# Retention and SoLU block on one Trainium2 core: state products as 64x64 tiles in two ordered passes, column means from fp32 column tiles, and a new written-out order

## Chip, cores and metric

The kernel runs on one core of one Trainium2 chip. The metric is the device time of one execution in microseconds (us). The kernel before was run three times: 220.96, 221.63 and 221.78 us, median 221.63 us.

## What is computed

```
q, k, v: [8 batches, 8 heads, 576 positions, 64], fp32
scores = (q @ k^T) / 8
ret    = scores * gamma_h ** (i - j)   for i >= j, else 0      gamma_h = 1 - 2 ** (-5 - h)
x      = (ret @ v), heads side by side                         [4608 tokens, 512]
h      = x @ w_in                                              [4608, 1024]
solu   = h * softmax(h)
ln     = (solu - mean) / sqrt(var + 1e-6) * g_ln               per token
out    = ln @ w_out                                            [4608, 512], fp32
```

The first half is causal attention with a decay for each head and no softmax, so what lies further back than the present window can be carried in a state of 64 x 64 numbers a head. The second half is a layer of two matrix products with SoLU and a layer norm between them. The mean of the layer norm is taken out of `w_out` (its columns are centred with weights `g_ln`), so that a token needs only its scale at the end.

## The kernel before

**Work units.** A window is 256 positions of one batch, or the last 64 positions of four batches (every ninth window). A window has two halves of four heads each; `i` numbers these 36 halves. A window gives two tiles of 128 tokens; `t` numbers these 36 tiles. Every step has a short name, and the engines execute these names in an order written out by hand in `ORDER` (L37 to L106), one string for each engine:

- SyncE (SP in the profile) issues all loads and stores: `ldq`, `ldk`, `ldv` (a quarter of a MB each; in the last windows four DMAs each), `lwi` (w_in) and `lwo` (w_out), `out` (two stores a tile, four in the last windows).
- GpSimd (POOL) scales and casts: `sq`, `sk` (L327), `cv` (L335), and keeps the states: `sm` (L458), `sc` (L467), and the scale of a token `rs` (L544, L545).
- TensorE: `T` transposes q and k into `ps["b"]`, `S` makes scores in `ps["a"]` (L402), `K` makes k^T v in columns 256 to 383 of `ps["x"]`, `I` adds what the state gives to columns 0 to 255 of `ps["x"]` and `V` adds what the window gives (all three end in `mm`, L368). `M1` is the product with w_in into `ps["h"]` (L483), `L` transposes solu into `ps["b"]` (L298, L552), `M2` is the product with w_out (L574). It writes the first half of `ps["a"]` for even tiles and the second for odd ones.
- VectorE: `mask` (L433), `sa` and `sd` (L447 to L454, states out of PSUM), `so` (solu, L510 and L515), `bn` (variance of even tiles), `wc` (centred w_out, L632).
- ScalarE: `qe` and `le` (transposes out of PSUM, L356 to L362, L561 to L563), `xe` (x out of PSUM, L473), `ex` (exponential, L501), `vs` (variance of odd tiles, L530), `oe` (result out of PSUM with its scale, L582), and `wg` (w_out times `g_ln` in fp16, L623, once for each of 8 chunks).

**PSUM.** There are four tiles of two banks: `h`, `a`, `b` and `x`. `h` holds one `M1` at a time, so the chain `M1`, `ex`, `so`, next `M1` runs in turn. `S` and `M2` share `a`.

**State products.** A state is kept as a 128 x 128 block-diagonal matrix for a pair of heads (`sbd`, zeroed off the diagonal at the start). `inter` (step `I`) multiplies it with 128 x 128 weights: two matmuls for the first window of a batch, four for the second, eight of 64 columns for the shared last window.

**Column means of w_out.** `WM` multiplies the eight fp16 chunks `w2g16` by a matrix of -1/1024 and accumulates (8 matmuls of 512 columns, L629); `wc` then reads the mean out of `ps["b"]`.

**Emission.** `order_ops` is a planner that walks the written orders with the costs in `DUR` and gives each step a planned start. The instructions are then emitted in the order of these planned starts; the semaphore waits follow from that program order. While TensorE has nothing to do before time `WARM`, `stir` (L745) fills in matmuls of zeros.

Of the kernel before, what the change touches and what calls it, by code (L numbers as in the profile page):

```python
# [9 lines left out]
FP = mybir.dt.float32  # L10
F16 = mybir.dt.float16
P = 128


DUR = dict(
    T=0.26, L=0.26, Tf=0.45, M1=1.73, M1a=1.3, M1b=0.44, M2=1.73, I=0.23, S=0.23, V=0.225, K=0.13, G=0.1, WM=1.73,
    qe=0.6, le=0.6, xe=0.61, ex=1.16, oe=0.72, vs=1.3, q2=0.24, wi=0.64, wib=0.5, wg=0.66, wgd=0.55, wc=0.66,
    cva=0.62, mask=1.24, sa=0.31, sd=0.31, so=1.26, sox=1.34, bn=1.64, sqd=0.72, gc=0.2,
    sq=1.06, sk=1.06, sm=0.42, sc=0.86, rs=1.0, cv=0.63,
    ld=0.5, ld4=2.6, ldw=0.6, out=1.1, out4=2.2, outz=0.55, lm=0.5,  # L20
)
MOVE = dict(ld=0.91, ld4=0.91, ldw=1.3, out=1.1, out4=1.1, outz=1.1, lm=0.4)
COUNT = dict(T=64, L=64, S=32, V=32, K=32, I=8, G=2, M1a=12, M1b=4)
# [4 lines left out]
START = dict(SP=2.3)  # L28
DMA_LAT, DMA_END = 0.1, 1.4
WARM = 31.0  # L30
NQ, NL = 9, 4
CA = (0,1,2,3,4,5)
WA = (0,1,2,3,4,5,6,7)
# [5 lines left out]
        "K0 G T0 S0 I0 V0 K1 T1 S1 I1 V1 T2 K2 S2 T3 I2 V2 K3 M1a S3 M1_0 I3 V3 K4 T4 M1_1 S4 I4 "  # L39
        "L0 V4 T5 L1 K5 S5 T6 M1_2 S6 I5 V5 K6 WM M1_3 I6 V6 K7 T7 S7 M1_4 T8 L2 M2_0 L3 M1_5 "  # L40
        "M2_1 I7 V7 K8 L4 T9 S8 M1_6 M2_2 I8 V8 K9 L5 T10 S9 M1_7 M2_3 I9 V9 K10 L6 S10 T11 M1_8 "
        "M2_4 I10 V10 K11 T12 L7 S11 M1_9 M2_5 I11 V11 K12 L8 S12 T13 M1_10 M2_6 I12 V12 K13 T14 "
        "L9 S13 M1_11 M2_7 I13 V13 K14 T15 S14 L10 M1_12 M2_8 I14 V14 K15 L11 T16 S15 M1_13 M2_9 "
        "I15 V15 T17 L12 S16 M1_14 M2_10 I16 V16 T18 L13 S17 M1_15 M2_11 I17 V17 K18 T19 S18 L14 "
        "M1_16 M2_12 I18 T20 V18 K19 L15 S19 M1_17 M2_13 I19 V19 K20 L16 T21 S20 M1_18 M2_14 I20 "
        "V20 L17 K21 T22 S21 M1_19 M2_15 I21 V21 K22 L18 T23 S22 M1_20 M2_16 I22 V22 L19 K23 T24 "
        "S23 M1_21 M2_17 I23 V23 K24 L20 T25 S24 M1_22 M2_18 I24 V24 T26 K25 L21 S25 M1_23 M2_19 "
        "I25 V25 K26 L22 T27 S26 M1_24 M2_20 I26 V26 K27 T28 L23 S27 M1_25 M2_21 I27 V27 K28 L24 "
        "S28 T29 M1_26 M2_22 I28 V28 T30 K29 L25 S29 M1_27 M2_23 I29 V29 K30 L26 S30 T31 M1_28 "
        "M2_24 I30 V30 K31 L27 T32 S31 M1_29 M2_25 I31 V31 K32 L28 S32 T33 M1_30 M2_26 I32 V32 "  # L50
        "K33 L29 T34 S33 M1_31 M2_27 I33 V33 L30 T35 S34 M1_32 M2_28 I34 V34 L31 S35 M1_33 I35 "
        "L32 V35 M2_29 L33 M1_34 M2_30 M2_31 L34 M1_35 M2_32 M2_33 L35 M2_34 M2_35"
    ),
    ACT=(
        "cv0 qe0 cv1 qe1 cv2 xe0 wi2a qe2 xe1 wi1a wi0a cv3 qe3 wi3a cv4 xe2 ex0 xe3 wg6 wg7 qe4 "
        "wg1 ex1 le0 cv5 wg0 qe5 le1 xe4 wg4 qe6 wg5 wg3 wg2 ex2 vs1 xe5 q20 ex3 qe7 vs3 ex4 le2 "
        "q21 xe6 qe8 oe0 le3 ex5 oe1 xe7 vs5 qe9 ex6 le4 oe2 q22 qe10 xe8 le5 ex7 oe3 xe9 le6 vs7 "
        "ex8 qe11 oe4 qe12 xe10 le7 ex9 oe5 xe11 q23 qe13 le8 ex10 q24 oe6 vs9 xe12 le9 ex11 qe14 "
        "oe7 xe13 qe15 le10 ex12 q25 oe8 vs11 qe16 xe14 ex13 le11 oe9 xe15 qe17 vs13 ex14 le12 "
        "oe10 xe16 q26 qe18 le13 ex15 oe11 xe17 qe19 le14 ex16 q27 oe12 vs15 xe18 qe20 ex17 le15 "  # L60
        "oe13 xe19 le16 vs17 ex18 qe21 oe14 q28 qe22 xe20 le17 ex19 oe15 xe21 qe23 le18 q29 ex20 "
        "oe16 vs19 xe22 qe24 ex21 le19 oe17 xe23 vs21 le20 ex22 qe25 oe18 qe26 q210 xe24 le21 "
        "ex23 q211 oe19 xe25 qe27 vs23 ex24 le22 oe20 qe28 le23 xe26 ex25 oe21 xe27 q212 le24 "
        "vs25 ex26 qe29 oe22 le25 xe28 qe30 ex27 oe23 xe29 q213 vs27 qe31 ex28 le26 oe24 le27 "
        "xe30 qe32 ex29 oe25 xe31 qe33 vs29 ex30 le28 oe26 le29 qe34 q214 xe32 ex31 oe27 xe33 "
        "le30 qe35 ex32 oe28 le31 xe34 ex33 le32 xe35 q215 oe29 vs31 ex34 le33 oe30 vs33 oe31 "
        "q216 ex35 q217 le34 oe32 vs35 oe33 le35 oe34 oe35"
    ),
# [722 lines left out]
```

## Time and profile before

| | |
|---|---|
| runs | 220.96, 221.63, 221.78 us; median 221.63 |
| the profiled execution | 221.71 us; span of its instructions 219.6 us; the rest lies around the span |
| busy share of the span | TensorE 92%, ScalarE 72%, GpSimd 65%, VectorE 64% |
| mean granted TensorE clock | 0.992 |
| instructions of the program | 10216 |
| read from HBM, written | 32.71 MB, 9.44 MB |

Times in the profile are microseconds from the start of the span. In the groups of the page a line reads: source line, engine, operation, output and input names, shapes, count; then busy time and mean ns of one; then the idle time of the engine before these instructions and what ended it. A matmul's duration there is its latency; how fast matmuls follow each other is read from their starts in the timeline. `PEld` is the weight load, which runs beside the matmuls. A name with q behind an engine (`SPq`) is a DMA issued by that engine.

### The profile page before, as it was taken

The page shows a single profiled execution, that of the slowest core. Times are in us where ns is not written, and L with a number is a line of the kernel's source. Part 1 is how long each engine was busy: PE and PEld are TensorE (multiplying, and loading weights), DVE is VectorE, ACT ScalarE, POOL GpSimd, SP SyncE. Part 2 cuts the span into 40 slices and gives each one's busy share as a digit, 9 for nine tenths or more (in the row PEclk, how much of TensorE's full clock was granted, in tenths as well). Part 3 has the DMA queues.
Part 4 walks back from the last instruction along what each step waited for, and adds up shares of the span by engine and source line. Part 5 has one row for each costly group of instructions (what it writes and reads, how often), then busy time and mean ns, then how long its engine had stood idle before and what let it go on. Part 6 is the DMA issues. An engine that isn't in the chain of part 4 may idle for free. (4 is left out here: it accounts for less than half of the span.)

```text
span 219.6 us, 10216 instructions
## 1 busy us (share of the span) xinstructions
PE 201.2 (92%) x4408; PEld 113.4 (52%) x4408; DVE 141.5 (64%) x238; ACT 157.5 (72%) x308; POOL 142.6 (65%) x237
## 2 busy tenths in 40 slices
PE   7967879699999999999989999999999999999860
PEld 3435454455555555566545555555555665554320
DVE  6266767896759685674865478677886685834400
ACT  3056789487877787897778779887878687676651
POOL 1196786995689786787769579889798477101110
PEclk9999999999999999999999999999999999999996
DMA  6999999965985557498988938896254454212443
GB/s 182 298 369 330 333 308 299 297 170 148 284 262 132 130 128 221 114 292 237 315 231 263 279 88 236 248 292 183 51 146 122 124 137 110 59 42 51 96 96 96
DMA packets 65644, 42.80 MB, mean 195 GB/s; under 512 B 4024, under 2 KB 59456, under 8 KB 65600
## 3 DMA queue, kind: packets, MB, share of 16 engines
q1 hardware_dynamic: 65200, 41.96, 68.6%
q8 instruction: 34, 0.56, 1.1%
q10 hardware_dynamic: 400, 0.21, 0.3%
q14 instruction: 10, 0.08, 0.1%
HBM read 32.71 MB, written 9.44 MB: 192 GB/s over the span
## 5 line engine op out<-in xcount | busy, mean ns | idle before, releaser
L483 PE MATMUL psh<-w_in,xT 128*128 128x512 f16 x288 | 68.9, 380 | 1.2 <-issue 1.0
L574 PE MATMUL psa<-w2c,lnT 128*128 128x512 f16 x288 | 67.7, 379 | 2.3 <-ACT lnT L563 1.3
L433 DVE TENSOR_TENSOR ret<-psa,masks 128x1024 f16<-128x1024 f32 x36 | 44.0, 1222 | 19.3 <-PE psa L402 15.7
L501 ACT ACTIVATE e_sb<-psh 128x1024 f32<-128x1024 f32 x36 | 36.8, 1022 | 16.0 <-PE psh L483 15.5
L574 PEld LDWEIGHTS <-lnT 128*128 128x128 f16 x288 | 28.0, 98 | 36.3 <-ACT lnT L563 1.7
L327 POOL TENSOR_TENSOR k<-kr,small 128x512 f16<-128x512 f32 x36 | 37.7, 1054 | 12.9 <-PE psx L368 6.4
L483 PEld LDWEIGHTS <-xT 128*128 128x128 f16 x288 | 25.2, 98 | 29.9 <-issue 2.4
L582 ACT ACTIVATE o_sb<-psa,rs 128x512 f32<-128x512 f32 x36 | 24.6, 686 | 18.6 <-issue 7.7
L327 POOL TENSOR_TENSOR q<-qr,small 128x512 f16<-128x512 f32 x34 | 35.1, 1041 | 2.4 <-DMA qr<-in_q_dram 1.6
L510 DVE SCALAR_TENSOR_TENSOR solu<-psh,e_sb 128x1024 f16<-128x1024 f32 x18 | 22.0, 1223 | 18.2 <-ACT e_sb L501 18.2
L515 DVE TENSOR_TENSOR solu<-psh,e_sb 128x1024 f16<-128x1024 f32 x18 | 22.0, 1222 | 15.1 <-ACT e_sb L501 15.0
L458 POOL TENSOR_TENSOR g<-tt,small 128x128 f32<-128x128 f32 x32 | 13.0, 406 | 25.0 <-DVE tt L454 23.4
L467 POOL CAST sbd<-g 64x256 f16<-64x256 f32 x64 | 25.3, 395 | 3.2
L521 DVE BATCH_NORM_STATS2 bs<-solu 128x6 f32<-128x512 f16 x36 | 22.9, 678 | 0.0
L473 ACT CAST xT<-psx 128x512 f16<-128x512 f32 x36 | 21.0, 585 | 1.1 <-PE psa L402 0.5
L530 ACT ACTIVATE junk<-solu,s 128x1024 f16<-128x1024 f16 x18 | 20.7, 1148 | 0.6
L563 ACT COPY lnT<-psb 128x512 f32<-128x512 f32 x32 | 18.7, 585 | 2.4 <-PE psb L298 2.3
L335 POOL CAST v<-vr 128x512 f16<-128x512 f32 x30 | 18.1, 609 | 1.3 <-DMA vr<-in_v_dram 0.9
L362 ACT COPY qkT<-psb 128x512 f32<-128x512 f32 x27 | 15.7, 583 | 3.9 <-PE psb L298 3.8
L402 PE MATMUL psa<-qkT 64*64 64x128 f16 x576 | 15.4, 220 | 3.2 <-ACT qkT L356 2.9
L544 POOL TENSOR_TENSOR w<-q,mv 128x2 f32<-128x2 f32 x18 | 3.5, 194 | 21.8 <-ACT junk L530 15.4
L368 PE MATMUL psx<-ret,v 64*64 64x128 f16 x576 | 15.0, 221 | 2.3 <-DVE ret L433 2.3
(56 smaller groups left out, 237.0 us busy)
## 6 DMA issues: line engine op xcount, KB each, us to landing
vr<-in_v_dram SPq DMA_DIRECT2D x32, 256.0 KB, 5.0
kr<-in_k_dram SPq DMA_DIRECT2D x32, 256.0 KB, 5.4
qr<-in_q_dram SPq DMA_DIRECT2D x32, 256.0 KB, 5.2
out_dram<-o_sb SPq DMA_DIRECT2D x64, 128.0 KB, 3.9
w_in_f<-in_moe_w_in_dram SPq DMA_DIRECT2D x4, 512.0 KB, 9.9
w_f<-in_moe_w_out_dram SPq DMA_DIRECT2D x4, 512.0 KB
qr<-in_q_dram SPq DMA_DIRECT2D x16, 64.0 KB, 3.6
kr<-in_k_dram SPq DMA_DIRECT2D x16, 64.0 KB, 3.3
```

The lines of the kernel that those rows point to most:

```text
L327: eng.tensor_tensor(out=t.rearrange("p j h d -> p h j d"), in0=st[i][nm + "r"], in1=g_of(i, base), op=ALU.mult,)
L433: nc.vector.tensor_tensor(out=d["ret"].rearrange("p e h j q -> p (e h) (j q)"), in0=ps["a"].rearrange("p e (h x) -> p (e h) x", h=2), in1= ...
L467: nc.gpsimd.tensor_copy(out=s16[ee[e], :, :, ee[e]], in_=st[i]["g"][ee[e]])
L473: nc.scalar.copy(out=d["xT"].rearrange("p c h q -> p c (h q)"), in_=ps["x"][:, :, 0:256])
L483: nc.tensor.matmul(out=h_ps[:, half_], lhsT=st[2 * w + dc // 2]["xT"][:, c, dc % 2], rhs=w_in16[:, dc, 512 * half_ : 512 * half_ + 512], s ...
L501: nc.scalar.activation(out=d["e"], in_=hh(t), func=ACT.Exp, accum_out=ws[w]["se"][:, c : c + 1])
L510: nc.vector.scalar_tensor_tensor(out=d["solu"], in0=hh(t), scalar=1.0, in1=d["e"], op0=ALU.mult, op1=ALU.mult, accum_out=d["s1"][:, 0:1],)
L515: nc.vector.tensor_tensor(out=d["solu"], in0=hh(t), in1=d["e"], op=ALU.mult)
L521: nc.vector.bn_stats(out=bs[:, x], in_=tk[t]["solu"][:, x * 512 : x * 512 + 512])
L530: nc.scalar.activation(out=junk, in_=d["solu"], func=ACT.Square, bias=d["s1"][:, 1:2], scale=1.0 / 32, accum_out=ws[w]["mv"][:, c, 1:2],)
L574: nc.tensor.matmul(out=oo(t), lhsT=d["lnT"][:, c].rearrange("p r q -> p (r q)"), rhs=w2c16[:, c], start=(c == 0), stop=(c == 7),)
L582: nc.scalar.activation(out=d["osb"], in_=oo(t), func=ACT.Copy, scale=ws[t // 2]["rs"][:, t % 2 : t % 2 + 1],)
```

## The change

- **State products.** A state is stored as it is (`s16`, 128 partitions x 2 x 2 x 64, from a pool), with one cast in `sc` in place of two, and no zeroed matrices. `inter` is called twice, as step `J` (the rows of the array that write the other bank) and step `I` (the rows that write the bank that `V` will write from there). Each call has 64 x 64 weights: two, four or eight matmuls. `V` takes its heads crosswise (`e ^ hp`), and w_in's odd chunks are loaded with their halves exchanged (two DMAs each).
- **Order of the passes.** A step `Z` lies between `J` and `I`: a `nop` on GpSimd (for i under 9) or SyncE (from 9 on) waits for `J`'s last matmul, and the first matmul of `I` waits for the `nop`.
- **Column means.** `gsh` holds g_ln times -1/1024. `WM0` and `WM1` multiply it with w_out in fp32, four chunks each into four column tiles of 32; `wp` (ScalarE) copies the partial sums to SBUF, `WS` adds and spreads them with an fp32 matmul, `wm` (ScalarE) copies the mean to SBUF, where `wc` reads it. The eight `wg` and the 13 VectorE memsets of `share` and `sbd` go.
- **End.** `M1_34` writes `ps["x"]`. The last tile's product is made in two halves of 256 columns, `M2_35` in `ps["h"]` and `M2_36` in `ps["a"]`, each with its own `oe` and stores.
- **Emission.** A TensorE step is emitted by its planned start as before; a step of another engine as soon as what it needs (its inputs, its buffers, the step before it on its engine) has been emitted.
- **Orders.** All five strings are written anew, and some planner costs with them.

The core of the diff (declarations and most of the order strings left out):

```diff
-    def inter(i):
+    def inter(i, near):
...
-        for c in range(2):
-            for hp in range(2):
-                for r in range(2 if wi == 2 else 1):
+        for hp in range(2):
+            for r in range(2):
+                c = r if near else 1 - r
+                e = r ^ hp
+                for x in range(2 if wi == 2 else 1):
...
-                    mm(d["begun"], c, 0, out=oo, lhsT=s16[:, hp], rhs=d["qkT"][:, c, 0, hp, :, qq])
+                    m = mm(d["begun"], c, e, out=xy[ee[e], c, hp, :, qq], lhsT=s16[ee[r], hp],
+                           rhs=d["qkT"][ee[r], c, 0, hp, :, qq])
+                    if near and "apart" in d:
+                        tc.add_manual_dep(m.ins, d.pop("apart"), SYNC)
+        if not near:
+            d["far"] = m.ins.name
+    def apart(i):
+        m = (nc.sync if i >= NZ else nc.gpsimd).nop()
+        tc.add_manual_dep(m.ins, st[i]["far"], SYNC)
+        st[i]["apart"] = m.ins.name
...
-        for e in range(2):
-            nc.gpsimd.tensor_copy(out=s16[ee[e], :, :, ee[e]], in_=st[i]["g"][ee[e]])
+        s16 = pools[f"s16{wi}"].tile([P, 2, 2, D], F16, tag="s16", name="s16")
+        nc.gpsimd.tensor_copy(out=s16, in_=st[i]["g"])
...
-    def w2_sum():
-        for x in range(8):
-            nc.tensor.matmul(out=ps["b"][:, 1], lhsT=share, rhs=w2g16[:, x], start=(x == 0), stop=(x == 7))
+    def w2_sum(k):
+        for x in range(4 * k, 4 * k + 4):
+            n = x % 4
+            nc.tensor.matmul(
+                out=ps["b"][32 * n : 32 * n + 32, 1], lhsT=gsh[:, x : x + 1].to_broadcast([P, 32]), rhs=w2_f[:, x],
+                start=(k == 0), stop=(k == 1), tile_position=(0, 32 * n),
+            )
+    def w2_spread():
+        nc.tensor.matmul(out=ps["b"][:, 1], lhsT=spread32, rhs=part, start=True, stop=True)
...
+    def cut(t):
+        if t < NT - 1:
+            return oo(t), t, slice(0, DM)
+        return (oo(t), NT - 1, slice(256, DM)) if t == NT else (ps["h"][:, 0], t, slice(0, 256))
...
+        key, made, used, eng = {}, {c: [] for c in caps}, {}, {}
         for o in sorted(ops, key=lambda o: start[o.name]):
+            near = [eng.get(o.eng, 0.0)] + [key[d] for d in o.deps]
...
+            key[o.name] = eng[o.eng] = start[o.name] if o.eng == "PE" else max(near) + 1e-7
...
+        for o in sorted(ops, key=lambda o: key[o.name]):
```

Four places of the new orders that the text below speaks of:

```
TensorE   ... V4 WM0 WM1 K5 WS M1_2 ...   V9 K10 T11 M2_2 M1_7 S11 J10 ... T12 M2_3 M1_8 M2_4 J11 ...
          ... K13 M1_10 M2_6 M2_7 M2_8 J13 ...   M1_20 M2_18 L19 J23 T25 I23 V23 K24 S24 M1_21 M2_19 J24 L20 T26 I24 ...
          ... L32 M1_33 M1_34 M2_31 L33 M1_35 L34 M2_32 M2_33 M2_34 L35 M2_35 M2_36
ScalarE   ... cv5 wp q20 vs1 wm ex2 ...   qe12 le6 ex8 oe3 oe4 ...   oe5 vs7 vs9 ex10 oe6 le8 q24 xe12 qe14 oe7 oe8 ...
          ... ex33 oe30 ex34 q216 oe31 le33 vs33 ex35 le34 oe32 q217 vs35 oe33 oe34 le35 oe35 oe36
SyncE     ... ldv4 ldk5 ldq5 lwo4 lwo0 lwo2 lwo6 ldv5 ...   ldq14 ldk14 Z9 ldv14 ldv15 ldq15 ldk15 ldq16 Z10 out1 ...
          ... Z17 ldq23 ldk23 ldv23 out11 Z18 ...
```

## The prediction

> **What bounds the kernel now.** I read the page first (busy shares and the 40 slices of 5.49 us), then a table by stage, the groups by shape, and the timelines of single stretches.
>
> ```profile
> PE 201.2 (92%) x4408; PEld 113.4 (52%) x4408; DVE 141.5 (64%) x238; ACT 157.5 (72%) x308; POOL 142.6 (65%) x237
> ...
> PE   7967879699999999999989999999999999999860
> ...
> GB/s 182 298 369 330 333 308 299 297 170 148 284 262 132 130 128 221 114 292 237 315 231 263 279 88 236 248 292 183 51 146 122 124 137 110 59 42 51 96 96 96
> ```
>
> TensorE is the only engine near full, and full from about slice 9. The table by stage (length, then each engine's busy time) says it more sharply:
>
> ```profile
> 20.00:30.00 10.00, 7.87 (x145) 4.65 (x149) 7.81 (x14) 8.77 (x17) 6.67 (x11) 1.00 1.09 311
> 160.00:180.00 20.00, 20.00 (x524) 11.70 (x522) 14.48 (x25) 16.05 (x32) 14.55 (x26) 1.00 0.52 133
> 200.00:210.00 10.00, 8.99 (x101) 4.09 (x100) 4.50 (x9) 6.36 (x14) 0.88 (x2) 1.00 0.25 59
> ```
>
> Three stages, then: a start with holes (to 47 us), a middle in which TensorE is busy 20.00 of 20 us, an end with holes. In the middle only what TensorE executes or waits for counts; GpSimd's 14.55 and VectorE's 14.48 are covered.
>
> **State products.** One cycle of the middle, TensorE's timeline (start, length, count):
>
> ```profile
> 164.90 0.39 PE L368 MATMUL psx<-qkT,sbd 128*128 128x128 f16 x4
> 165.21 0.42 PE L368 MATMUL psx<-ret,v 64*64 64x128 f16 x16
> 165.46 0.29 PE L368 MATMUL psx<-v,k 64*64 64x64 f16 x16
> ```
>
> The 4 full products start within 0.39-0.22 = 0.17 us, 0.056 each; `I` takes 4 x 0.056 = 0.224 and then 0.09 until `V` starts, when the shape changes. `V`'s 16 tiles run four at once: 0.25 us for four slots, 0.056 each and 0.024 more for the first. The new `J` and `I` fill one slot each where four tiles are free: 0.080 + 0.056, and `V` loses its first-slot surcharge. Second windows (16 halves): 0.224 + 0.248 before, 0.080 + 0.056 + 0.224 after, 0.112 us less. Shared windows (4 halves, 8 products of 64 columns, a slot of 0.032): about the same, 0.11. First windows (16): 2 x 0.056 before, two half-filled slots after: nothing. Sum 20 x 0.11 = 2.2 us less. There are as many shape changes as before, two a cycle. The casts (395 ns each, 32 fewer) leave GpSimd, which is covered.
>
> Against this stands the new wait. `J` ends 0.24 us after its start (latency in the rows above); the hop to the next engine and back is at least twice 0.05 and a nop, 0.12 in all by the ACT-to-PE gaps (0.05). So `I` may start 0.36 after `J`. For even halves `L` and `T` lie between (0.08 + 2 x 0.25 = 0.58): covered. For odd halves only `T` (0.33): 0.05 short with prompt queues, times 18 is 0.9; the weights of `I` cannot be loaded ahead of the wait, 0.024 x 36 = 0.9. Net gain 2.2 - 1.8 = 0.4 us. Bounds: 2.2 if nothing shows; minus 4 if the hop costs 0.4 in place of 0.12.
>
> The row first: `V`'s concurrent tiles of the two row halves write different banks and start within 0.01 us. The Trainium skill (PSUM — Partial Sum Buffer, PSUM bank collisions) says that different row tiles may not write one bank at the same time and that software must keep them apart; this speaks against one joint pass and is why the wait cannot be had for nothing. By a joint pass the term would be the full 2.2 us.
>
> The nop sits in SyncE's queue behind DMA issues, so a late SyncE holds TensorE:
>
> ```profile
> 90.10 2.26 SPq L312 DMA_DIRECT2D kr<-in_k_dram  x1
> 92.41 0.50 SPq L312 DMA_DIRECT2D qr<-in_q_dram  x1
> ...
> 96.29 2.53 SPq L312 DMA_DIRECT2D qr<-in_q_dram  x1
> 98.91 1.42 SPq L593 DMA_DIRECT2D out_dram<-o_sb  x2
> ```
>
> [...] Between two steps `Z` of the middle lie three loads and a store, 3 x 0.76 (mean) + 1.2 = 3.5 of 5.0 us: in time. From `Z9` to `Z10` lie four loads and four small ones of 0.62: 5.5 us against 4.8 of TensorE work. I charge 0.7 us once; bounds 0 and 5.
>
> **Pairs of out products.** The new emission puts each `oe` ahead of the next `M2`. What that does is seen at the end of the trace:
>
> ```profile
> 201.59 0.69 ACT L582 ACTIVATE o_sb<-psa,rs 128x512 f32<-128x512 f32 x1 [1.91 <-issue]
> 203.55 0.67 ACT L582 ACTIVATE o_sb<-psa,rs 128x512 f32<-128x512 f32 x1
> ...
> 213.84 1.26 ACT L582 ACTIVATE o_sb<-psa,rs 128x512 f32<-128x512 f32 x2 [2.04 <-issue]
> ```
>
> ```profile
> 197.89 3.62 PE L574 MATMUL psa<-w2c,lnT 128*128 128x512 f16 x16
> 204.27 3.61 PE L574 MATMUL psa<-w2c,lnT 128*128 128x512 f16 x16 [0.56 <-ACT o_sb L582]
> 211.85 1.90 PE L574 MATMUL psa<-w2c,lnT 128*128 128x512 f16 x8 [1.25 <-ACT lnT L563]
> ```
>
> `oe30` reads the first half of `ps["a"]`, complete at 199.8, yet starts at 201.59, when `M2_31` in the other half ends (201.51). `M2_32` needs only `oe30`'s half, yet starts 0.05 us after `oe31` ends (204.22). `oe34` starts when `M2_35` ends. So the two halves are guarded as one: whichever is emitted later waits. Before, ScalarE waited, which cost little; now TensorE will wait for ScalarE, wherever no `S` stands between two `M2`.
>
> - `M2_4` behind `M1_8`: `oe3` stands behind `ex8`, which starts when `M1_8` ends. Latency 0.17 + `ex` 1.22 + `oe` 0.69 less overlap: 2.0 us.
> - `M2_7` waits for `oe6` and `M2_8` for `oe7`: 0.17 + 0.09 + 0.69 + 0.05 = 1.0 us each.
>
> All lie in the full middle: 4.0 us. Bounds: 0, if TensorE waits there for something else anyway, and 5.
>
> **Start.** The first real product comes at 9.58 us, after 31 matmuls of zeros, though its inputs are there at 6.3; the new order starts `T0` near 6.4, and third and fourth halves are done 4 us sooner. Then the load order binds. Up to `lwo6` lie 18 loads of 0.262 MB, masks and 4.19 MB of weights: 9.05 MB. By the slices 8.3 MB are moved at 27.45 us, so it is there at 30, and `ldv5` behind it at 31, with landing 32. ScalarE's order has `cv5` before `wp`: 0.6 + 0.6, then `WS`, then `M1_2` at 34.4 (before: 33.33). From there `M1`, `ex`, `so` (1.9 + 1.2 + 1.2 + 0.1) give `M1_3` at 38.8, `M1_4` at 43.2; `ex4` stands behind `qe8` and `le2`, so `M1_5` at 49.5 (before 49.21). By then `I7 V7 K8 S8`, 0.8 us of TensorE, are done in addition. Net 0.5 us gained. Of the removed `wg` (5.5 us ScalarE) about 1 us was on the path, before `ex2`; the `wc` (5.5 us VectorE) stay.
>
> No row shows an fp32 matmul over 8 columns. By the nearest, L629's eight at 0.217 apart (1.73 us), two rounds of four at once and the spread cost between 0.65 and, all nine in turn at a latency of 0.38, 3.4 us; I take 2.8, since two conversions of the sum lie between. FP8 and Floating Point Precision (Trainium skill, TensorE Precision Notes) gives four passes for true fp32: an estimate of 3 x 4 x 0.217 = 2.6 us, and the total would stand 0.2 lower.
>
> **End.** From the start of `M1_33` (191.28) to the end of the span (219.62) it takes 28.3 us; `M2_29`, `M2_30` and a block (4.05 us) lie ahead of it in the new order, so 24.3 compare. New: three products to 5.5 (0.3 for `oe30`), `L33`, `M1_35` to 7.7, `M2_32` to 10.1, 0.8 for `oe32`, `M2_33` to 12.8, `oe33` after `vs35`, `M2_34` to 15.5, `le35` after `oe34` 16.9, the halves to 18.8, `oe36` 19.3. The last store is issued at 20.6 behind SyncE's four and four of 0.43, landing 1.26 and close 1.54 as before: 23.4. Gain 0.9 us; bounds 2.5 and -1.
>
> **Sum.** The profiled execution took 221.71 us, 0.08 above the median. 221.7 - 0.4 + 0.7 + 4.0 - 0.5 - 0.9 = 224.6, on the median 224.5 us.
>
> **Rivals.** A (forecast, 0.50): as above; with its bounds 222 to 227.
> B (0.32), faster: the head start of 3.2 us and the 0.9 at `ex2` reach the middle, because the weights land sooner than I have them. Then the start gives 5.3 in place of 0.5: 219.7 us. For it speaks that ScalarE is busy 8.77 of 10 us from 20 to 30 and loses 5.5 us of `wg`; against it that transfers run at 330 GB/s up to 33 us and are the same in sum. It decides from 4.5 us on: `M1_5` before 45.5. With the best bounds of products and end, 217.5.
> C (0.13), slower: the nops are late in each cycle by some 0.2 us: 27 x 0.2 = 5.4 more, 230. SyncE's 2.5 us issues speak for it, its slack of 1.5 us a cycle against it.
> D (0.05): the four tiles of a pass do not run at once, each costs a slot: 6 x 0.056 x 20 = 6.7 us more, 231. `V`'s rows speak against it.
>
> Differences within 0.5% (220.5 to 222.7) cannot be told from no change. A gives 0.08 there and 0.42 above, C and D 0.18 above, B 0.02 there and 0.30 below: faster 0.30, same 0.10, slower 0.60. The range leaves out the top of C and D and the bottom of B: 218 to 229; A alone 222 to 227.
>
> **What would show it.** `M2_4` with idle time of 2 us ended by `o_sb`; two more of 1 us at `M2_7` and `M2_8`; `J` and `I` starting within 0.01 us for four matmuls; `M1_5` between 48 and 51; the waits of L368 on SyncE near zero, except near `Z10`. Wrong if TensorE shows no wait on `o_sb` there, or if `M1_5` starts before 46.

## The result, and the profile after

The changed kernel took 228.81 us in the median of four runs (228.02 to 230.58), the kernel before 221.30 us on the same chip: a ratio of 1.036 (95%: 1.028 to 1.043). The profiled execution took 228.02 us, its span is 226.2 us against 219.6, so 6.6 us more where I had 2.9. In the experiments below the ratios compare executions within 1.5% of the fastest of their kernel, while the medians are of all executions, and a profile can be that of the fastest (e8_pairs, 224.7 us; e18_tail, 218.3) or the slowest one (e14_znop_all, 226.4).

The page of the changed kernel, with the same two lines as before and the granted clock:

```profile
PE 203.7 (90%) x4542; PEld 110.5 (49%) x4542; DVE 137.8 (61%) x227; ACT 155.5 (69%) x303; POOL 130.3 (58%) x204
...
PE   7688588789997897999999999999999999999861
...
PEclk9955799999999999999999999999999999999999
...
GB/s 187 300 318 241 298 318 272 293 290 228 143 196 144 88 154 128 126 242 287 283 197 211 224 214 196 199 259 207 250 240 92 162 106 6 49 142 47 51 107 78
```

TensorE has full slices (5.65 us each) from the 10th on, loses some in the 13th, 14th and 16th, and is full throughout only from the 17th (before: from the 9th). In the fourth slice the loads move 241 GB/s (330 before), and TensorE runs at half clock; it does so from 11.5 to 21.8 us and from 25.2 to 28.6. The table by stage, same stretches as before:

```profile
20.00:30.00 10.00, 7.10 (x79) 3.24 (x77) 3.42 (x7) 5.07 (x9) 2.07 (x5) 0.74 1.06 295
160.00:180.00 20.00, 19.46 (x536) 10.95 (x535) 13.74 (x24) 16.48 (x33) 15.66 (x25) 1.00 0.66 185
200.00:210.00 10.00, 9.95 (x167) 4.90 (x166) 7.34 (x12) 8.23 (x18) 0.89 (x2) 1.00 0.33 77
```

From 20 to 30 us ScalarE is busy 5.07 us in place of 8.77. Part of that is the removed `wg`, but it also waits for data. Its timeline names its four casts of w_in, and `cv5`, which the column means wait for:

```profile
20.84 0.62 ACT L628 CAST w_in<-w_in_f 128x512 f16<-128x512 f32 x1 [2.64 <-DMA w_in_f<-in_moe_w_in_dram]
...
23.14 0.62 ACT L628 CAST w_in<-w_in_f 128x512 f16<-128x512 f32 x1 [1.20 <-DMA w_in_f<-in_moe_w_in_dram]
...
25.14 0.62 ACT L628 CAST w_in<-w_in_f 128x512 f16<-128x512 f32 x1 [0.90 <-DMA w_in_f<-in_moe_w_in_dram]
27.29 0.62 ACT L628 CAST w_in<-w_in_f 128x512 f16<-128x512 f32 x1 [1.52 <-DMA w_in_f<-in_moe_w_in_dram]
...
35.83 0.62 ACT L336 CAST v<-vr 128x512 f16<-128x512 f32 x1 [1.00 <-DMA vr<-in_v_dram]
```

A chunk of w_in lands every 2 us or so, and the load behind `cv5` lands just before 35.83, where the forecast had 32; `M1_0` ends at 28.85 us (23.73 before) and `M1_5` starts at 54.73 (49.21).

The state products, in TensorE's timeline of one cycle of the middle:

```profile
162.27 0.22 PE L369 MATMUL psx<-qkT,s 64*64 64x128 f16 x2
...
162.59 0.24 PE L369 MATMUL psx<-qkT,s 64*64 64x128 f16 x2
162.60 0.46 PE L369 MATMUL psx<-ret,v 64*64 64x128 f16 x16
```

`J` and then, 0.32 us later, `I`; `V` follows within 0.01 us. That is a first window, with two products each. In a second window, with four:

```profile
172.09 0.23 PE L369 MATMUL psx<-qkT,s 64*64 64x128 f16 x4
...
172.43 0.25 PE L369 MATMUL psx<-qkT,s 64*64 64x128 f16 x4
172.51 0.39 PE L369 MATMUL psx<-ret,v 64*64 64x128 f16 x16
```

The four products of `I` hold `V` up by 0.08 us in all. TensorE's timeline at `M2_4`, `M2_7` and `M2_8`:

```profile
74.47 1.89 PE L587 MATMUL psa<-w2c,lnT 128*128 128x512 f16 x8 [1.78 <-ACT o_sb L597]
87.31 1.89 PE L587 MATMUL psa<-w2c,lnT 128*128 128x512 f16 x8 [0.83 <-ACT o_sb L597]
89.97 1.89 PE L587 MATMUL psa<-w2c,lnT 128*128 128x512 f16 x8 [0.78 <-ACT o_sb L597]
```

With the product's own latency these are 1.94, 0.99 and 0.94 us beyond the usual spacing, as forecast. In TensorE's waits, `o_sb` stands first, and the nop on SyncE (L401) far below it:

```profile
PE psa L587 <- ACT o_sb L597: 5.0, 5, 1.8
...
PE psx L369 <- SPq L401: 1.1, 3, 0.5
```

(total us, times, longest). So the middle and the end look like the forecast, and the start does not.

### The profile page after: what moved, and what is told of

Same layout as the page of the kernel before. It is cut to its first block, busy times and chain, and to the rows that moved or that the text cites. A ratio compares the mean times of both kernels' runs of the same rounds, so it can differ in the third digit from the quotient of the medians.

```text
span 226.2 us, 10443 instructions
## 1 busy us (share of the span) xinstructions
PE 203.7 (90%) x4542; PEld 110.5 (49%) x4542; DVE 137.8 (61%) x227; ACT 155.5 (69%) x303; POOL 130.3 (58%) x204
## 4 chain that ended last, share of the span: by engine, by line
PE 53%; DMA 13%; SPq 10%; POOL 8%; ACT 6%; issue 5%; DVE 3%; POOLq 0%; ACTq 0%; DVEq 0%
PE psa L587 20%; PE psh L491 19%; PE psx L369 5%; PE psb L299 5%; DMA w_in_f<-in_moe_w_in_dram 5%; SPq L313 5%; DMA qr<-in_q_dram 4%; SPq L609 3%; DMA vr<-in_v_dram 3%; PE psa L413 3%; ACT o_sb L597 2%; SPq L320 2%; POOL q L328 2%; DMA out_dram<-o_sb 2%; DVE ret L444 1%
## 5 line engine op out<-in xcount | busy, mean ns | idle before, releaser
L587 PE MATMUL psa<-w2c,lnT 128*128 128x512 f16 (+1 forms) x288 | 67.2, 376 | 5.7 <-ACT o_sb L597 5.0
L491 PE MATMUL psh<-w_in,xT 128*128 128x512 f16 x280 | 67.9, 385 | 0.8 <-ACT w_in L628 0.6
L509 ACT ACTIVATE e_sb<-psh 128x1024 f32<-128x1024 f32 x35 | 35.8, 1023 | 20.6 <-PE psh L491 20.5
L587 PEld LDWEIGHTS <-lnT 128*128 128x128 f16 x296 | 28.5, 98 | 39.8 <-issue 7.5
L491 PEld LDWEIGHTS <-xT 128*128 128x128 f16 x288 | 26.0, 98 | 31.4 <-issue 3.1
L597 ACT ACTIVATE o_sb<-psa,rs 128x512 f32<-128x512 f32 (+1 forms) x36 | 24.5, 680 | 19.0 <-PE psa L587 13.0
L523 DVE TENSOR_TENSOR solu<-psh,e_sb 128x1024 f16<-128x1024 f32 x17 | 20.8, 1222 | 18.5 <-ACT e_sb L509 18.4
L529 DVE BATCH_NORM_STATS2 bs<-solu 128x6 f32<-128x512 f16 x36 | 22.9, 679 | 0.0
L369 PE MATMUL psx<-qkT,s 64*64 64x128 f16 (+1 forms) x256 | 17.9, 229 | 4.1 <-POOL s L475 2.0
L336 POOL CAST v<-vr 128x512 f16<-128x512 f32 x30 | 18.7, 626 | 0.0
L369 PEld LDWEIGHTS <-s 64*64 64x64 f16 x256 | 8.7, 105 | 16.0 <-issue 4.6
```

The source lines that it names most:

```text
L369: m = nc.tensor.matmul(start=(c, e) not in begun, stop=False, skip_group_check=True, **kw)
L491: nc.tensor.matmul(out=h_ps[:, half_], lhsT=st[2 * w + dc // 2]["xT"][:, c, dc % 2], rhs=w_in16[:, dc, 512 * half_ : 512 * half_ + 512], s ...
L509: nc.scalar.activation(out=d["e"], in_=hh(t), func=ACT.Exp, accum_out=ws[w]["se"][:, c : c + 1])
L523: nc.vector.tensor_tensor(out=d["solu"], in0=hh(t), in1=d["e"], op=ALU.mult)
L529: nc.vector.bn_stats(out=bs[:, x], in_=tk[t]["solu"][:, x * 512 : x * 512 + 512])
L587: nc.tensor.matmul(out=o[:, cols], lhsT=tk[t]["lnT"][:, c].rearrange("p r q -> p (r q)"), rhs=w2c16[:, c, cols], start=(c == 0), stop=(c = ...
```

## Experiments

Positions are starts of steps in the profiled execution of each kernel. Each was timed beside the kernel before:

| kernel | median us | ratio to the kernel before (95%) | `M1_5` | `M1_33` | span |
|---|---|---|---|---|---|
| before | 221.3 | 1 | 49.21 | 191.28 | 219.6 |
| after | 228.8 | 1.036 (1.028 to 1.043) | 54.73 | 203.03 | 226.2 |
| e1_stir | 229.3 | 1.034 (1.024 to 1.044) | 55.23 | 203.39 | 226.6 |
| e2_whole | 227.1 | 1.021 (1.014 to 1.028) | 50.86 | 202.48 | 225.4 |
| e3_emit | 229.0 | 1.029 (1.020 to 1.038) | 55.61 | 203.80 | 227.2 |
| e4_oldstate | 229.7 | 1.033 (1.026 to 1.040) | 51.44 | 204.88 | 227.8 |
| e5_swap | 226.4 | 1.021 (1.015 to 1.027) | 51.57 | 201.56 | 224.5 |
| e6_actq | 230.4 | 1.037 (1.030 to 1.044) | 55.30 | 205.83 | 229.0 |
| e7_znop | 224.6 | 1.015 (1.008 to 1.021) | 50.95 | 199.87 | 222.9 |
| e8_pairs | 227.4 | 1.021 (1.013 to 1.030) | 51.17 | 200.03 | 222.9 |
| e9_lag | 228.2 | 1.024 (1.015 to 1.034) | 51.67 | 196.52 | 224.7 |
| e10_combo | 223.8 | 1.010 (1.001 to 1.020) | 52.35 | 200.85 | 223.8 |
| e11_ex4 | 232.5 | 1.050 (1.044 to 1.057) | 55.85 | 207.88 | 230.8 |
| e12_oldstate2 | 231.7 | 1.048 (1.042 to 1.054) | 52.72 | 206.82 | 229.7 |
| e13_nomean | 227.7 | 1.019 (1.010 to 1.029) | 52.38 | 203.95 | 226.8 |
| e14_znop_all | 223.5 | 1.004 (0.999 to 1.009) | 52.25 | 201.43 | 224.3 |
| e15_s8 | 227.2 | not settled (224.2 to 229.0 us) | 54.48 | 200.67 | 223.6 |
| e16_before64 | 225.9 | 1.015 (1.007 to 1.023) | 53.96 | 195.10 | 223.3 |
| e17_products | 228.6 | 1.029 (1.023 to 1.036) | 51.55 | 196.09 | 224.8 |
| e18_tail | 220.3 | 0.995 (0.991 to 0.999) | 49.08 | 189.08 | 216.5 |

### The start: clock or loads

**e1_stir**: `int((start - end_pe - 0.3) / 0.36)` becomes `int((start - end_pe - 0.1) / 0.24)` in the number of zero products.

> The changed kernel with more matmuls of zeros in the planned gaps of the first 31 us (one for each 0.24 us of a gap in place of one for each 0.36 us less 0.3). Theory L (the start is late because the loads land late): the weights of M1_0 still land at 27.3 us, so M1_0 ends within 0.7 us of 28.85, M1_5 starts at 54.7 within 0.7, and the time is that of the changed kernel within 0.8 us. Theory C (the start is late because TensorE runs at half clock from 11 to 25 us): the granted clock is 0.9 or more there, M1_0 ends at 26.5 or sooner, M1_5 starts 2 to 3 us sooner, the time falls by 2 to 3 us.

The clock is full but for one slice:

```profile
PEclk9999699999999999999999999999999999999999
```

`M1_0` ends at 28.97 (28.85), `M1_5` starts 0.5 us later, the time is the same. Theory C falls: taking the long stretch at half clock away gains nothing, since `M1_0` waits for w_in either way. A short stretch is left in both kernels (24.3 to 27.7 us here, 25.2 to 28.6 there). In the changed kernel the last two products of `M1_0` take 0.89 us in it, and 0.61 at full clock here: 0.3 us at most.

**e2_whole**:

```diff
-        for r in range(2 if c % 2 else 0):
-            nc.sync.dma_start(out=w_in_f[ee[r], c], in_=w_in_v[ee[1 - r], c])
-        if c % 2 == 0:
-            nc.sync.dma_start(out=w_in_f[:, c], in_=w_in_v[:, c])
+        nc.sync.dma_start(out=w_in_f[:, c], in_=w_in_v[:, c])
```

> The changed kernel with every chunk of w_in loaded by one transfer of 128 rows; the exchange of the two row halves in the odd chunks is left out, so the hidden layer sees the features of odd chunks in another order. Theory L, with the transfers of 64 rows as its cause: w_in's last chunk lands 2 us or more sooner (before 25.3 us in place of 27.3), 0.5 MB more are moved by 24 us, M1_5 starts 2 to 3 us sooner and the time falls by 2 to 3 us. If the lateness comes from the place of w_in in the queue or from the clock: w_in lands within 0.7 us of 27.3, M1_5 within 0.7 of 54.7, the same time.

(The planner's cost of these loads changes with them.) The last cast of w_in starts at 22.86 in place of 27.29, `M1_0` ends 4.7 us sooner, `M1_5` starts 3.9 us sooner. `cv5` starts where the forecast had the landing of its load:

```profile
31.86 0.62 ACT L336 CAST v<-vr 128x512 f16<-128x512 f32 x1 [1.04 <-DMA vr<-in_v_dram]
```

The table from 18 to 26 us (last column GB/s, before it the busy share of the DMA engines), first of the changed kernel, then of this one:

```profile
18.00:26.00 8.00, 5.72 (x107) 3.54 (x108) 3.00 (x6) 3.02 (x6) 2.79 (x4) 0.71 1.09 254
```

```profile
18.00:26.00 8.00, 6.02 (x82) 2.71 (x80) 4.50 (x10) 5.46 (x10) 3.36 (x6) 1.00 1.08 363
```

The DMA engines are as busy in both, and move 254 against 363 GB/s: the packets take longer. In the DMA records the 4 KB packets of the 128-row chunks take 0.164 us in the median, those of the 64-row halves about 0.30. But of 3.9 us at `M1_5` only 0.6 are left at `M1_33`. TensorE's timeline shows where they went:

```profile
165.67 0.25 PE L369 MATMUL psx<-qkT,s 64*64 64x128 f16 x4 [1.20 <-SPq L401]
...
177.52 0.24 PE L369 MATMUL psx<-qkT,s 64*64 64x128 f16 x2 [1.83 <-SPq L401]
```

That is the mechanism of rival C of the prediction, at two places and not in each cycle, and only once TensorE is ahead.

**e5_swap** keeps the exchange of the row halves, in the casts: for odd chunks `copy(out=w_in16[ee[r], c, cols], in_=w_in_f[ee[1 - r], c, cols])` for `r` in 0, 1.

> The changed kernel with every chunk of w_in loaded by one transfer of 128 rows, and the exchange of the two row halves of the odd chunks made by their casts (two casts of 64 rows each in place of one of 128). Theory L (64-row transfers make the weights late): M1_5 starts at 51 to 52.2 (50.86 as in e2_whole, plus up to 1.2 for two more casts of 0.62 us on ScalarE), against 54.73 in the changed kernel; the time is 227.1 to 228.3, as in e2_whole or a little more. If e2_whole won by something else in its wrong order of features: M1_5 within 0.7 us of 54.73.

`M1_5` at 51.57, 3.2 us sooner, and 1.5% less time than the changed kernel by the two ratios: theory L holds with the full computation.

**e6_actq**: `(nc.scalar if r else nc.sync).dma_start(out=w_in_f[ee[r], c], ...)`.

> The changed kernel with the second 64-row half of each odd chunk of w_in issued by ScalarE's queue, the first by SyncE's as before, so that both halves are under way together. In the changed kernel the 4 KB packets of the odd chunks take 0.30 us each, those of the even chunks 0.164 us. Theory H (64 rows at a time can be written only at about half the rate; both halves together run at the full one): the packets of the odd chunks fall to 0.16 to 0.2 us, 18 to 26 us move over 320 GB/s in place of 250, M1_5 starts 2 to 4 us sooner. Rival: a transfer of 64 rows is slow by itself, whatever runs beside it: packets stay near 0.3, M1_5 within 1 us of 54.7.

Packets of the odd chunks stay near 0.31 us. From 18 to 26 us:

```profile
18.00:26.00 8.00, 5.64 (x115) 3.85 (x119) 3.81 (x7) 3.80 (x8) 3.74 (x7) 0.71 1.09 251
```

251 GB/s, and `M1_5` starts at 55.30. But the halves were not under way together, as was meant. The timeline of the two queues:

```profile
6.24 1.17 ACTq L619 DMA_DIRECT2D w_in_f<-in_moe_w_in_dram  x2
...
15.80 1.23 SPq L619 DMA_DIRECT2D w_in_f<-in_moe_w_in_dram  x1
```

In the DMA records the 4 KB packets of ScalarE's queue run from 9.6 to 13.1 us, those of SyncE's from 17.6 on. The first take 0.32 us in the median with no other 4 KB packet beside them: a transfer of 64 rows is slow by itself, as the rival says. Whether two halves at once run at the full rate (theory H) was not tested.

**e16_before64** makes the one edit in the kernel before: `for r in (ee if c % 2 else [slice(0, P)])`: `dma_start(out=w_in_f[r, c], in_=w_in_v[r, c])`.

> The kernel before, with the odd chunks of w_in loaded as two transfers of 64 rows (each row to its own place; same bytes, same order of loads). Theory L: packets of these chunks take 0.30 us in place of 0.164, the last chunk lands 2.5 to 4 us later, M1_0 ends 2.5 to 4 us later than 23.73, M1_5 starts 2 to 4 us later than 49.21, and the time is 1.5 to 3.5 us above the kernel before. If the lateness of the changed kernel came from its order of loads: M1_5 within 1 us, time within 0.8 us.

`M1_0` ends 4.9 us later (28.61), `M1_5` 4.75 us later, the ratio is 1.015 (1.007 to 1.023), some 3.3 us. Its table:

```profile
18.00:26.00 8.00, 4.84 (x84) 2.61 (x83) 4.34 (x9) 3.95 (x7) 3.19 (x7) 0.77 1.12 259
```

259 GB/s, with the old order, the old products and the old emission. This one edit gives nearly the delay at `M1_5` by which the whole change missed its forecast there (4.75 and 5.2 us). Not all of it is the loads' own: the last cast of w_in ends 3.6 us later (26.14, 22.55 before), and from there to the end of `M1_0` it takes 1.3 us more, at half clock (its products start 0.43 us apart, 0.22 before).

**e13_nomean** (on e5_swap): `WM`, `wp`, `WS`, `wm` left out, `mean` set to zero.

> As e5_swap, without the column means: WM, wp, WS and wm are left out and the mean is set to zero, so the hidden layer's mean is not taken from the output. My sum had 2.8 us for the chain. Theory M (the means are on the path): M1_2 starts at 32.4 to 33 in place of 34.84 (then bound by so1), M1_5 1.5 to 2.5 us sooner, time 1.5 us or more less. Rival: others bind M1_3 to M1_5 (qkT of ScalarE, ret of VectorE): M1_2 sooner, M1_5 by less than 0.7 us.

`M1_2` at 34.48, `M1_5` at 52.38, the time not below e5_swap: the rival by its wording. But `M1_0` ended late in this execution (27.66, 25.53 in e5_swap), by 0.5 us because the last cast of w_in ended later and by more because it ran at half clock (3.60 us in place of 2.16). Counted from its end, `M1_2` comes 2.5 us sooner and `M1_5` 1.3. That would fit the 2.8 us I had for the chain, with half or less of it reaching the middle; one execution does not settle it.

**e11_ex4** and **e15_s8**, on the rest of the start:

```diff
e11  ACT  -vs3 qe8 le2 ex4     +vs3 ex4 qe8 le2
     DVE  -mask8 sa8 so4 sd8   +sa8 sd8 so4 mask8
e15  PE   -T8 L2 J7 S8 I7 V7 K8 L3 M2_0 M1_5   +T8 J7 L2 I7 V7 K8 L3 M2_0 S8 M1_5
     ACT  -vs3 qe8 le2 ex4     +vs3 le2 ex4 qe8   (DVE as in e11; nops as in e14_znop_all)
```

> As e5_swap, with ex4 ahead of qe8 and le2 on ScalarE and so4 ahead of mask8 on VectorE, nothing else. M1_4 ends at 46.4 there and ex4 starts only behind qe8 and le2. Theory Q (this queue place is what is left of the late start): M1_5 starts 1.5 to 2.5 us sooner than in e5_swap (49 to 50 in place of 51.57), M1_12 keeps 1 us or more of it. Rival: the scores S8 then come later and M1_6 waits as long: M1_6 within 0.5 us of e5_swap.

> As e14_znop_all, with S8 behind M2_0 (on TensorE), ex4 ahead of qe8 and so4 ahead of mask8. In e11_ex4 M2_0 waited 2.5 us for mask8, as S8 stood ahead of it and they share banks. Theory Q2 (without that, ex4's place is worth its 1.7 us): M1_5 starts at 49.5 to 50.3, the time is 1 to 2 us below e14_znop_all. Rival (S8 is then late for V8, mask8 for M2_1): M1_6 within 0.5 us of e14_znop_all.

Both fail. In e11 `M1_5` starts at 55.85, 4.3 us later, because `M2_0` stands ahead of it and shares its banks with `S8`, whose reader `mask8` now comes later:

```profile
52.50 3.52 PE L587 MATMUL psa<-w2c,lnT 128*128 128x512 f16 x8 [2.51 <-DVE ret L444]
```

After that wait of 2.51 us `M2_0` runs at half clock (0.50 from 52.4 to 55.8 us) and takes 3.52 us in place of 1.89. In e15, with `S8` behind `M2_0`, `M1_5` still starts at 54.48 (52.35 in e10_combo, whose order is the same up to there but for these edits): now transposes wait 1.64 us for `qkT`, the state products 1.18 for GpSimd and `S8` 0.82 for `o_sb`. `ex4`'s place is held by several chains at once; what is left of the late start stays open.

### The pairs of out products

**e3_emit**: `sorted(ops, key=lambda o: key[o.name])` becomes `key=lambda o: start[o.name]`, as before.

> The changed kernel with its operations written out in the order of their planned starts, as in the kernel before; each engine's own order is untouched. Theory P (two out products in a row wait for o_sb because the first one's reader is now written ahead of the second): the gaps of 1.94, 0.99 and 0.94 us at M2_4, M2_7 and M2_8 go, TensorE's idle time on o_sb falls from 5.0 to about 1, the time falls by 3.9 us to 225. Rival G (the gaps are given back: ScalarE, which then waits, is late for what follows, or loads are late anyway): M2_12 comes no more than 1.5 us sooner after M1_5 than in the changed kernel, and the time falls by 1.5 us at most.

The three gaps go, and `M1_5` to `M1_12` takes 42.84 us in place of 43.50: 0.7 us of 3.9. Rival G: ScalarE now waits until a pair's second product ends and is late with `le8` (89.12 us, 87.16 before), so `M2_8` waits 1.30 us for `lnT`; scores wait 0.5 us for `o_sb`. A wait of 0.9 us put down to issue, which the changed kernel has not, takes part of the gain too.

**e8_pairs** (on e5_swap), by order alone:

```diff
 ACT  -ex8 oe3                      +oe3 ex8
 PE   -M1_10 M2_6 M2_7 M2_8 J13 ... K14 S14 M1_11 M2_9 J14 ... K15 S15
      +M1_10 M2_6 J13 ... K14 M2_7 S14 M1_11 M2_8 J14 ... K15 M2_9 S15
```

> As e5_swap, and the out products taken apart by order alone: oe3 ahead of ex8 on ScalarE; M2_7, M2_8 and M2_9 one each behind K14, M1_11 and K15, with their oe in step. Theory P (three gaps of 3.9 us in all are work that TensorE loses): none of the three gaps, M1_5 to M1_12 takes 39.6 to 40.5 us in place of 43.5, the time falls by 3 to 4 us against e5_swap, less what the nops on SyncE take back. Rival G (as e3_emit showed: other waits take their place): M1_5 to M1_12 takes over 42 us, with new idle time of TensorE on lnT, qkT or s in that stretch.

44.99 us where 39.6 to 40.5 was expected (44.06 in e5_swap). `M2_4`'s gap is gone (`M1_8` to `M1_9` 4.9 us in place of 6.85); the other two come back as waits of the scores, which share the banks, and of the state products:

```profile
83.14 0.24 PE L369 MATMUL psx<-qkT,s 64*64 64x128 f16 x2 [1.88 <-ACT xT L481]
...
87.48 0.42 PE L413 MATMUL psa<-qkT 64*64 64x128 f16 x16 [0.78 <-ACT o_sb L597]
95.81 0.42 PE L413 MATMUL psa<-qkT 64*64 64x128 f16 x16 [1.38 <-ACT o_sb L597]
```

**e9_lag** (on e5_swap, with `oe3` ahead of `ex8`) does not catch up at all: `M2_7`, `M2_8` leave the cycle of `M2_6`, each later product, with its `oe` and `out`, stands two places later.

> As e5_swap, with oe3 ahead of ex8, and without catching up: M2_7 and M2_8 are not done in one cycle with M2_6, every later out product stands two places later (M2_9 at M1_13, as in the kernel before), the last two at the end. Theory P2 (three out products in one cycle share their banks with the scores and cost their work and 1 us each; at the end they fill holes): against e5_swap M1_33 starts 6 to 7.5 us sooner (two products of 1.73 and gaps of 3.9 less), M1_33 to the end takes 26 to 28 us in place of 22.9, and the time falls by 2 to 4 us. Rival N (the nops behind SyncE take every head start): M1_33 starts less than 4 us sooner and the time is within 1 us of e5_swap.

`M1_33` starts 5.0 us sooner, and from there it takes 28.2 us in place of 22.9: the span is the same within 0.2 us. Both theories are wrong in part. The catch-up costs what it saves at the end, since every pair at the end waits for its `oe` in the same way (1.29, 0.83, 0.78 us there).

### State products and nops

**e4_oldstate** puts the block-diagonal products back (`inter`, `av`, `state_cast` and `sbd` of the kernel before; `J` and `Z` gone; w_in in whole chunks); **e12_oldstate2** the same with `I` in `J`'s place.

> The changed kernel with the block-diagonal state products of the kernel before (four products of 128x128 at I's place, two casts for each state, no J, no nop, w_in loaded in whole chunks), all other orders and edits kept. To be set against e2_whole, which shares its loads. My sum: the 64x64 tiles gain 2.2 us and lose up to 1.8 by the wait, so this kernel is 0.4 slower than e2_whole. If the wait shows only where it is visible in the trace (1.1 us on SyncE), it is 1 to 2.5 us slower than e2_whole; a cycle of the middle (M1_21 to M1_25) takes 20.2 us in place of 19.8 for four. If the wait costs more than the tiles gain, it is faster than e2_whole by 1 us or more.

> The changed kernel with the block-diagonal state products of the kernel before at J's place, directly behind an out product (no I, no nop; w_in in whole chunks). In e4_oldstate they stood at I's place, between 64x64 tiles, which adds two changes of shape a cycle, so that kernel overstated the price. Theory S (the 64x64 tiles gain 0.05 us a cycle on the mean, 0.09 for second windows and nothing for first ones): M1_12 to M1_25, 64.9 us in e2_whole, takes 65.3 to 66.0 here; there are no waits on SyncE, so the time is 225 to 226, below e2_whole. If the tiles gain what e4_oldstate seems to show (67.1 us): 66.8 or more. If the wait takes all: 64.9 or less.

Both are slower than e2_whole, by 1.2% and 2.7% of the ratios: e4 by 2.6 us, just over the most I had allowed, e12 by 4.6 us where I expected it to be faster. The order was made for `J` and `I`, so new waits come in: 3.5 and 3.6 us for the states (1.9 in e2_whole), and in e12 3.7 us of transposes waiting for `lnT`. In e4 the cycles behind 100 us show no wait and still take 5.1 to 5.3 us (4.9 in e2_whole): there the products stand between 64x64 tiles, with two more changes of shape. What the products themselves cost is read from cycles without a wait, by the starts of `M1`. e12, a second window (four products), then a first one (two):

```profile
122.93 1.90 PE L487 MATMUL psh<-w_in,xT 128*128 128x512 f16 x8
...
127.94 1.90 PE L487 MATMUL psh<-w_in,xT 128*128 128x512 f16 x8
...
133.82 1.90 PE L487 MATMUL psh<-w_in,xT 128*128 128x512 f16 x8
...
138.71 0.61 PE L487 MATMUL psh<-w_in,xT 128*128 128x512 f16 x2
```

and e2_whole, second then first:

```profile
125.30 1.90 PE L491 MATMUL psh<-w_in,xT 128*128 128x512 f16 x8
...
130.23 1.90 PE L491 MATMUL psh<-w_in,xT 128*128 128x512 f16 x8
...
135.13 0.39 PE L491 MATMUL psh<-w_in,xT 128*128 128x512 f16 x1
```

5.01 against 4.93 us, and 4.89 against 4.90. So 0.08 a cycle is gained for second windows, nothing for first ones, and the nop's hop is not seen in either.

**e7_znop** (on e2_whole): nops `Z27` to `Z35` on GpSimd. **e10_combo** (on e5_swap): the same and `oe3` ahead of `ex8`. **e14_znop_all**: as e10, all nops from `Z9`.

> As e2_whole (all w_in chunks in one transfer, the exchange of row halves left out), with the nops Z27 to Z35 on GpSimd in place of SyncE, at their planned places. In e2_whole the head start of 3.5 us at M1_25 is gone by M1_30, with idle time of 1.20 and 1.83 us on SyncE's nop. Theory N (the nop behind SyncE's stores and loads is what takes the head start): these two waits go, M1_25 to M1_30 takes 25.3 to 25.8 us in place of 28.3, the time falls by 2.5 to 3 us. Rival: TensorE meets another late work there (loads that come late, GpSimd's queue): M1_25 to M1_30 still takes 27 us or more and the time falls by less than 1 us.

> As e5_swap, with oe3 ahead of ex8 and the nops Z27 to Z35 on GpSimd. If the terms add: 1.9 us of M2_4's gap and 2 us of the nops less than e5_swap, M1_33 at 197.5 to 198.5, time 222.3 to 223, about that of the kernel before. If another nop on SyncE ahead of Z27 or GpSimd's queue takes the 1.9 us: M1_33 at 199.5 or later, time 224 or more.

> As e10_combo, with all nops from Z9 on GpSimd. e10_combo waited 2.8 us on SyncE's nops in four places. Theory N: these waits go, M1_33 starts at 198 to 199 in place of 200.85, time 221 to 222. Rival: GpSimd, whose operations take 0.4 to 1.04 us and wait for loads, holds more nops than SyncE: idle time of L369 on GpSimd of 2 us or more, time over 223.5.

In e7 the two waits go, `M1_25` to `M1_30` takes 24.65 us in place of 28.28, and the median falls by 2.5 us: theory N. One wait of 1.21 us comes in, at a nop that is still on SyncE (155.13 us). In e10 nops ahead of `Z27` wait (1.30 us at 101.41, 2.8 in all); `M1_5` to `M1_33` is 1.5 us shorter than in e5_swap, where 3.9 was the sum: the terms do not add. In e14 none is left on SyncE; its ratio of 1.004 (0.999 to 1.009) is that of the kernel before. So the change with its loads and nops mended, and `oe3` ahead of `ex8`, is level with the kernel before.

**e17_products**: the kernel before with the state products of the change alone (transposes between `J` and `I`, nops on GpSimd, exchange in the casts).

> The kernel before with the state products of the change alone: J at I's old place, the transposes of the cycle between J and I, I directly ahead of V, every nop on GpSimd, w_in loaded in whole chunks with the exchange of row halves in the casts of the odd chunks (four more casts). Theory S (0.09 us less in a cycle of a second or shared window, nothing for a first): 20 x 0.09 = 1.8 us less from M1_5 to the end, 0 to 1 us more at the start for the casts: 219.5 to 221.5 us. Rival W (I waits for GpSimd's nop where J to I holds only one or two transposes, 0.1 to 0.3 us a cycle): no gain or a loss, 222 us or more, with idle time of L368's products on GpSimd.

Slower by 2.9%. `M1_5` starts 2.3 us later (`M1_0` ends at 26.31: with four more casts the last ends 2.1 us later, and `M1_0` runs at half clock), and `M1_5` to `M1_33` takes 144.5 us in place of 142.1, with 2.4 us in which out products wait for the mask. Neither theory: TensorE's products show no wait on a nop, but VectorE's state steps wait 5.1 us in all for `xe`, which comes behind `V` (none in the kernel before), and they stand ahead of the masks. So I read it that moving `V` behind the transposes costs more than the 1.8 us of the tiles; no run tests this by itself.

### The end alone

**e18_tail**: the kernel before with

```diff
-        h_ps = ps["h"]
+        h_ps = ps["x" if t == NT - 2 else "h"]
 PE   -M2_29 L33 M1_34 M2_30 M2_31 L34 M1_35 M2_32 M2_33 L35 M2_34 M2_35
      +M2_29 M1_34 L33 M2_30 M1_35 M2_31 L34 M2_32 M2_33 L35 M2_34 M2_35 M2_36
```

and the halves of the last tile (`cut`), ScalarE's order in step.

> The kernel before with the end of the change alone: M1_34 written into the freed pair of banks of the window sums, M1_35 ahead of M2_31, the last tile's out product and its eviction in two halves, the first in a freed bank. Theory E (the end's holes close by this): nothing changes up to M1_33 at 191.3; from there to the end of the span it takes 26 to 27.3 us in place of 28.3, the time falls by 1 to 2 us (ratio 0.991 to 0.996). Rival: the chain exp, product, transposes, eviction of the last tile sets the end whatever the order: 28 us or more from M1_33, ratio 0.998 or above.

From `M1_33` to the end of the span 27.4 us (216.5 - 189.08) in place of 28.3, just over the 27.3 of theory E. Ratio 0.995 (0.991 to 0.999): the only version whose interval lies below the kernel before, by 0.5%. TensorE's timeline shows `M1_34` directly behind `M2_29`, in the window's banks, 4.4 us behind `M1_33` (4.9 before, behind `L33`):

```profile
193.48 1.89 PE L483 MATMUL psx<-w_in,xT 128*128 128x512 f16 x8
```

Ahead of `M1_33` nothing was changed, yet it starts 2.2 us sooner than in the profiled execution of the kernel before, 1.5 of them between `M1_15` and `M1_21`, where that one waits 1.0 us on issue. This is variation between executions; what counts is the 0.9 us behind `M1_33` and the ratio.

## Why the prediction was right or wrong

| term of the sum | predicted us | measured us |
|---|---|---|
| state products, tiles | -2.2 | -1.6 (an estimate, 20 x 0.08) |
| the wait for the nop | +1.8 | +1.1, SyncE late in three places; none in quiet cycles |
| SyncE late at `Z10` | +0.7 | none there |
| pairs of out products | +4.0 | +3.9 (1.94, 0.99, 0.94) |
| start | -0.5 | +4.7 |
| end | -0.9 | -1.1 |
| span | +2.9 | +6.6 |

The start is 54.73 - 49.21 - 0.8 for the work done ahead; the end 226.2 - 203.03 = 23.2 against the comparable 24.3. The middle, `M1_5` to `M1_33`, is 6.2 us longer; less the 4.05 moved into it, and with the 0.8 that was done ahead, +3.0 (forecast +4.3). The rows above it add to 3.4; the kernel before also lost 1.0 us there to waits put down to issue, which the changed kernel did not. The rest of some 0.6 us is not assigned.

**The failed step is the start**, and in it one sentence: "By the slices 8.3 MB are moved at 27.45 us, so it is there at 30, and `ldv5` behind it at 31, with landing 32." `cv5`, which waits for that landing, starts at 35.83. I took the rate of the old transfers for the new ones, as the bytes are the same. The diff, which front and prediction both had, splits two chunks of w_in into transfers of 64 rows. That I took for two more issues on SyncE. It is a lower rate: 254 GB/s from 18 to 26 us, against 334 in the kernel before and 363 in e2_whole. `M1_0` waits for all of w_in, and what stands behind it in the queue is about 4 us later too, `ldk5` (GpSimd waits for its load until 28.76), then `T5`, `ldv5`, `cv5` and `wp`. With whole transfers (e2_whole) `cv5` starts at 31.86, `M1_2` at 33.98 and `M1_3` at 38.84, where I had 34.4 and 38.8; in the changed kernel they start at 37.95 and 42.72. So the chain behind the loads was priced rightly up to there, and what went into it was late. e16_before64 shows that the edit by itself costs the kernel before 4.75 us at `M1_5`; e2_whole and e5_swap get 3.9 and 3.2 us of it back in the changed kernel. A second, smaller miss lies behind `M1_3`, with these loads or without: `M1_3` to `M1_4` takes 4.93 us where I had 4.4, and `M1_4` to `M1_5` 7.08 (7.09 in e2_whole) where I had 6.3. That is 1.3 of the 5.2 us; e11_ex4 and e15_s8 did not close it, and its cause stays open.

The Trainium skill has this rule: SBUF — State Buffer, Door 1 (the DMA port swizzle), says that the bandwidth of a transfer goes by how many of 16 ports its rows reach, and that rows 0 to 63 reach eight, so 64 rows load no faster than 32. The runs agree in direction (packets 0.30 us against 0.164). DMA: Bandwidth & Descriptors, Rules for kernel authors, adds that transfers to the two halves serialize, from one issuing engine or from two. No run here shows that, since in e6_actq the two queues moved their halves at different times. I had asked such rules about the products of this change and not about its loads.

**Rival B** had its condition the wrong way round: the weights land later, not sooner. (Its sum is off too: 3.2 and 0.9 us with the 0.5 of the forecast are 4.6, not 5.3.) **Rival C** is small in the changed kernel (1.1 us) and grows once something else is mended: with the start repaired, TensorE runs ahead of SyncE and loses 3.0 us at two nops (e2_whole), got back by e7_znop. **D** fell by the rows of the second window: four products in 0.08 us, where a slot each would take 0.22. The signs I had named, `M2_4` at 2 us, two more of 1 us, `J` and `I` paired, came as said. Near `Z10` there was no wait on SyncE, and the 1.1 us came at 103, 143 and 178 us; `M1_5` came at 54.7, outside 48 to 51 and on the side I had given no case to. That 228.8 us still lies within 218 to 229 is luck: the top of the range was there for C and D, and neither brought it.

**State products**: the tiles were sized somewhat high. The 1.8 us of the nop did not come as a hop in each cycle, but as 1.1 us where SyncE was late. In the nop's sum is a slip: 0.36 - 0.33 leaves the odd halves 0.03 us short, not 0.05, so 0.5 us and not 0.9.

**Pairs**: the size was right as idle time, but as a cost to be had back it was not: e3, e8 and e9 take the gaps away and get 0.7 us, nothing and nothing, because the scores share the banks and the end then pays. `M2_4`'s gap alone closes without a wait in its place (one swap on ScalarE); in e10_combo, which has that swap, nops on SyncE wait 0.85 and 0.33 us in the same stretch, and `M1_5` to `M1_12` is 0.6 us shorter than in e5_swap.

## What to carry to other kernels

A diff that keeps the bytes of a transfer and changes its rows changes its time: cost each changed DMA by its shape, not by the old rate, and ask first what the first weighted product waits for. An idle gap is not a price until a run without it is faster; here three ways of closing 3.9 us of gaps gave back less than one. A wait that is handed through a busy queue shows no cost while the waiting engine is late for another reason, and appears when that reason is mended.

## What the runs showed of the hardware beyond this

- Transfers of 64 rows by 4 KB take about 1.8 times the packet time of one of 128 rows (0.30 against 0.164 us; 0.32 on a queue of their own in e6_actq), with the DMA engines shown as equally busy (1.09 against 1.08).
- In the changed kernel TensorE's clock was 0.5 from 11.5 to 21.8 us, before w_in was there (matmuls of 512 columns 0.427 us apart in place of 0.217), and holding it at full speed there with zero products changed the time by nothing (e1_stir). Where nothing else is waited for it costs: in e11_ex4 `M2_0` took 3.52 us in place of 1.89.
- One fp32 product of 128 x 512 (`WS`) took 0.96 us from its start to the next product's, 4.4 times an fp16 one; the eight fp32 products on 32 columns each (`WM`) together 2.2 us, near two rounds of four at once (1.9) and far from eight in turn (7.7).
- With the same loads, the last cast of w_in ended between 23.9 and 25.4 us in eight kernels, and `M1_0` between 25.4 and 27.7: its eight products took 2.2 us at full clock (e5_swap) and 2.8 to 3.6 us where the clock was 0.5 for part or all of them. So a start moves from one execution to another by the loads and by the clock.
